# Routing half a chunk sooner, and the rows of the later dense groups mixed on other engines and turned in fp32r

## The chip, the cores and the metric

The kernel runs on one core of one Trainium2 chip. The metric is the device time of one execution in microseconds (us). Five engines run side by side, each with its own in-order queue: TensorE (PE, with its weight loads shown as PEld), VectorE (DVE), ScalarE (ACT), GpSimd (POOL) and SyncE (SP). Semaphores order them where one needs what another makes. DMAs are issued from the queues of SP, ACT and POOL.

## The reference

All in float32. Sliding-window attention of 4 batches, 8 heads, 576 positions and 64 values a head, so 2304 tokens of 512 values; then a layer of 8 experts, of which each token takes two; then a dense layer of two products with a gate between them.

```python
mask = (rel >= 0) & (rel < 64)                      # rel = query position - key position
x = softmax(where(mask, q @ k.T / 8, -1e9)) @ v     # -> x [2304, 512]
noisy = x @ w_gate + log1p(exp(x @ w_noise)) * noise
top2 = indices of the two largest of noisy; top2_w = their softmax
y[mask] += top2_w[mask, k] * (relu(x[mask] @ w1[e]) @ w2[e])     # for each expert e, k in (0, 1)
h = y @ w_in                                        # [2304, 2048]
g = where(h >= 1, h, where(h <= -1, 0, (h + 1) ** 2 / 4))
out = g @ w_out                                     # [2304, 512]
```

## The kernel before

Products are made in three fp32r matmuls: each operand is cut into a high half that fp32r holds and a low half with the rest, and high by high, low by high and high by low are summed in PSUM. A tile is typed fp32r or f32; PE transposes a tile in its own type. ACT copies the high half (`AF.Copy` into an fp32r tile) and DVE subtracts it for the low half: `split_w` and its second part `rest_w` for weights, `xpose` for rows of x.

The order of instructions is written out by hand; each engine's queue follows the order of the Python calls. There are three stages.

Attention and routing. `step(u)` runs for u = 0 to 36 (NU = 36), two steps for a tile of 128 tokens. It makes scores (`A`), a row maximum on DVE (`top`), exponentials on ACT (`soft`), transposes them (`C`), and every second step multiplies them with v (`Dm`), which ends with a normalization on DVE: `rl`, its reciprocal, and x = ov * rl (L406 to L409). Two steps later x is transposed (`Ex`) and the router's logits are made (`Gm`, in `logits`). Tiles are routed in groups of 8, 4 and 6. `route(g)` is a generator of many small DVE steps; `advance` lets each live one run to its next stop, and then makes up to 2 or 4 marks: for each choice a pair of one-hot tiles, `ohr` (L586) and `ohe` (L593 on DVE or L596 on ACT). `place` (L634) multiplies the pairs on PE into a PSUM bank that sums up each expert's list of tokens. As soon as the marks of the first two groups are placed, `early` reads that bank (L460 to L479), and POOL gathers the first three blocks of rows for expert 0 (`xg0a`, L732), so that expert 0 can start while the last six tiles are still being routed. `xpose` turns these rows (L759).

Experts. A unit is one expert, or for expert 0 two (`0a`, `0b`). Its eight chunks of 128 hidden values each have a first product (`do_mm1`, L891), a relu split into halves (ACT L899, DVE L902), and a second product (`do_mm2`, L964). The first product of the next chunk always stands ahead of the second product of this one. `rest = tail()` is the generator that finishes the routing of the last group beside expert 0: each call `more()` places what marks there are and advances `route(2)`; when all is placed it makes the lists, gathers the rows of `0b` and counts. The first four calls in the order before were: at the top of chunk 0, after the first product of chunk 1, after the second product of chunk 0, and at the top of chunk 1. The fifth, after the first product of chunk 2, issues the router's sums on PE (L558 to L562), which need `ohs` (L543).

Dense layer. Five groups of 2, 4, 4, 4 and 4 blocks of 128 tokens. `prep_gather` loads for each block the two rows that the experts made (y1, y2), the block is mixed as y1 * w0 + y2 * w1, turned by PE (`xturn`, L1236) and copied (`xcopy`, L1242). The first group uses plain products; the other four a Strassen scheme of seven products (`wino`, L1178), for which `xsums` makes four differences of quarters (L1255) and `xsplit` cuts seven operands into halves (L1265, L1267). The products go to two PSUM banks in turn; each is evicted by one or two DVE instructions, or one on ACT (L1159, L1163, L1168). `gate` follows (ACT L1196 and L1202, DVE L1197, L1200 and L1206). A group has eight items p, an item seven slots j; in slot (p, j) stand the j-th product of an item two ahead, a part of a gate and a seventh of the second products of this item. The preparation of the next group stands in slots named by hand. Groups 2, 3 and 4 are prepared under groups 1, 2 and 3, which are alike; group 1 is prepared under group 0, in another way that the diff leaves as it is.

Of the kernel before, what the change touches and what calls it, by code (L numbers as in the profile page):

```python
# [57 lines left out]
def fused_kernel(ctx, tc, qT, kT, v, wg, noise, wcat, out, wd=None):  # L58
# [617 lines left out]
    def step(u):  # L676
# [27 lines left out]
        if u % 2 == 1 and 0 <= m - 2 < NT:  # L704
            logits(m - 2, u)
        place()
        early()
        advance(MARKS[u > NU - 10])
        if 0 <= u - 1 < NU:
            Dm(u - 1)  # L710
# [40 lines left out]
    def xpose(key, b, m=P, TR=TR):  # L751
        if key not in xT:
            xT[key] = x_tiles(key, F32R)
        hi, lo = xT[key]
        t = gat.pop((key, b))

        o, i = (TR.bitcast(F32R), idr) if t.dtype == F32R else (TR, idn)
        for k in range(4):
            nc.tensor.transpose(o[:, k * P:k * P + m], t[0:m, k * P:k * P + P], i[0:m, 0:m])  # L759
        tv = TR.rearrange("p (k t) -> p k t", k=4)[:, :, 0:m]  # L760
        sl = slice(b * P, b * P + m)
        nc.scalar.activation(hi[:, :, sl], tv, AF.Copy)
        nc.vector.tensor_tensor(out=lo[:, :, sl], in0=tv, in1=hi[:, :, sl].bitcast(F32), op=ALU.subtract)
# [251 lines left out]
    def prep_gather(un, b):  # L1015
# [9 lines left out]
        else:  # L1025
            y = [pool["sc"].tile([P, DM], F32, tag="s", name=f"y{t}_{c}") for c in range(2)]
            eng = nc.gpsimd if un is units[FIRST2 + 1] else nc.sync
            for c in range(2):
                eng.dma_start(out=y[c], in_=yd[:, c, :])
        gat[un["key"], b] = (y, t)  # L1030

    def mix_two(un, b):
        (y1, y2), t = gat[un["key"], b]
        nc.scalar.activation(y1, y1, AF.Copy, scale=wts[:, t, 0:1])
        yield
        nc.vector.scalar_tensor_tensor(out=y2, in0=y2, scalar=wts[:, t, 1:2], in1=y1, op0=ALU.mult, op1=ALU.add)
        gat[un["key"], b] = y2

    def prep_mix(un, b):
# [190 lines left out]
    def xturn(ui, b):  # L1230
        un = units[ui]
        t = gat.pop((un["key"], b))
        free = [bank[7]] + [x for x in bank[2:7] if x not in units[ui - 1]["m2"]]
        held[ui, b] = to = free[b % len(free)]
        for k in range(4):
            nc.tensor.transpose(to[:, k * P:k * P + P], t[:, k * P:k * P + P], idn)  # L1236

# [7 lines left out]
    def xsums(ui, part=(0, 1, 2, 3)):  # L1245
# [7 lines left out]
        for i in part:  # L1253
            out, x, y = ((t1, b12, b11), (t2, b22, t1), (t3, b22, b12), (t4, b21, t2))[i]
            (nc.vector if d else nc.gpsimd).tensor_tensor(out=out, in0=x, in1=y, op=ALU.subtract)  # L1255
        if 3 in part:
# [27 lines left out]
    n64 = 2 * NF2  # L1284
    ndec = ndl = 0
    do_mm1(0)
    ndone = 1
    for s in range(len(seq)):
# [59 lines left out]
        if ui == 0:  # L1348
            more()
            if f == NF - 2:  # L1350
# [4 lines left out]
                rank(0)  # L1355
                prep_gather(units[2], 0)
                rank(1)
# [3 lines left out]
        do_mm2(s, ahead_xpose)  # L1361
        if s in (0, 2):
            rest_w(EW - 2 + s // 2, slice(0, 1024))
        if s == 0:
            more()
        for _ in range(SPLITS[ui][f] if ui in SPLITS else int(0 < ui < U7A)):
# [22 lines left out]
        if ui == U7B and f:  # L1389
# [4 lines left out]

    AT = ({(4, 0): (None,), (4, 4): (0,), (4, 5): (1,), (5, 0): (2,), (5, 1): (3,), (5, 3): (4,), (6, 2): (5,), (6, 3): (6,)},
          {})
# [13 lines left out]
    for q, (ui, p) in enumerate(items):  # L1410
# [22 lines left out]
        for j in range(7):  # L1433
            if nxt:
# [6 lines left out]
                if not late:  # L1441
                    if 1 <= p < 3 and j in (2, 4):
                        prep_mix(nxt, 2 * (p - 1) + j // 2 - 1)
                    if 2 <= p < 4 and j in (1, 3):
                        xturn(ui + 1, 2 * (p - 2) + j // 2)
                        xcopy(ui + 1, 2 * (p - 2) + j // 2)
                else:
# [6 lines left out]
                for x in AT[late].get((p, j), ()):  # L1454
                    xsums(ui + 1) if x is None else xsplit(ui + 1, x)
            if j < len(g):
# [40 lines left out]
```

## Time and profile before

| what | value |
|---|---|
| median of 3 runs | 954.07 us (952.11 to 954.48) |
| the profiled execution's own time | 953.95 us |
| its span, first to last instruction | 952.2 us |
| mean granted TensorE clock | 0.998 |
| PE busy | 938.4 us, 99% |
| DVE, ACT, POOL busy | 69%, 47%, 23% |

The span leaves out what lies before the first and behind the last instruction, 1.75 us here. Times in the rows count from the span's start. Busy time of PE is modelled at the ends of matmuls, so that a PE that is shown busy may still run below its rate; the distance from one start to the next tells more. In brackets stands how long the engine had been idle and what ended it.

### The profile page before, as it was taken

The numbers are of one execution on the slowest core, as the hardware profiler recorded it, in microseconds if no ns is written. First come the engines' busy times: TensorE is split into PE (matmuls) and PEld (weight loads), VectorE is DVE, ScalarE is ACT, GpSimd is POOL, SyncE is SP. The second block draws the span as 40 slices with busy tenths as digits, with TensorE's granted clock in tenths as the row PEclk, the third lists the DMA queues.
The fourth block names the chain that finished last, engine by engine and source line by source line (L and its number), as shares of the span: only waits on it lengthen the run. The fifth ranks groups of instructions, "written<-read, shape, count | busy, mean of one in ns | idle before, by whom it ended". The sixth has DMA issues, their size and how long they took to land. (4 is left out here: it accounts for less than half of the span.)

```text
span 952.2 us, 18037 instructions
## 1 busy us (share of the span) xinstructions
PE 938.4 (99%) x6779; PEld 832.8 (87%) x6781; DVE 659.5 (69%) x1386; ACT 444.3 (47%) x920; POOL 222.1 (23%) x273
## 2 busy tenths in 40 slices
PE   9999899999999999999999999999999999999998
PEld 6887788988889889889888889988998899899997
DVE  5688665477997968889543377766766777677664
ACT  7897325345565555555432366343334334442221
POOL 4222013133544353354402030013002201300000
PEclk9999999999999999999999999999999999999999
DMA  8884126555888777767626567775586458556521
GB/s 269 289 271 150 50 89 195 187 194 198 285 287 285 256 233 278 258 211 250 244 89 202 201 212 254 256 235 175 177 273 208 149 173 306 174 176 207 188 94 44
DMA packets 91274, 196.95 MB, mean 207 GB/s; under 512 B 7320, under 2 KB 18072, under 8 KB 91184
## 3 DMA queue, kind: packets, MB, share of 16 engines
q1 hardware_dynamic: 83152, 171.68, 54.4%
q0 software_dynamic: 6736, 21.86, 6.4%
q10 hardware_dynamic: 1296, 2.23, 0.6%
q8 instruction: 54, 0.88, 0.4%
q14 instruction: 36, 0.29, 0.1%
HBM read 155.45 MB, written 40.29 MB: 206 GB/s over the span
## 5 line engine op out<-in xcount | busy, mean ns | idle before, releaser
L964 PE MATMUL bank<-wo,hall 128*128 128x512 f32 x864 | 237.6, 394 | 0.0
L964 PE MATMUL bank<-w,hall 128*128 128x512 f32 (+3 forms) x944 | 236.2, 398 | 0.1
L964 PEld LDWEIGHTS bank<-w,hall 128*128 128x128 f32 (+3 forms) x944 | 168.8, 185 | 35.5 <-issue 0.3
L964 PEld LDWEIGHTS bank<-wo,hall 128*128 128x128 f32 x864 | 146.7, 188 | 17.4 <-DVE hall L910 0.2
L899 ACT ACTIVATE hall<-bank 128x288 fp32r<-128x288 f32 (+6 forms) x128 | 54.0, 422 | 219.7 <-PE bank L891 197.3
L891 PE MATMUL bank<-xhie,w 128*128 128x288 f32 (+4 forms) x768 | 122.6, 302 | 0.5 <-DVE hall L902 0.4
L891 PEld LDWEIGHTS bank<-xhie,w 128*128 128x128 f32 x768 | 113.5, 188 | 7.5 <-DVE hall L902 1.3
L902 DVE SCALAR_TENSOR_TENSOR hall<-bank,hall 128x288 fp32r<-128x288 f32 (+7 forms) x168 | 59.9, 390 | 84.3 <-ACT hall L899 76.2
L149 DVE TENSOR_TENSOR w<-raw,w 128x1024 fp32r<-128x1024 f32 (+1 forms) x69 | 82.0, 1188 | 23.7 <-ACT w L158 19.4
L1178 PEld LDWEIGHTS bank<-xb,wi 128*128 128x128 f32 x576 | 80.5, 188 | 10.1 <-DVE cg L1168 1.2
L1202 ACT ACTIVATE hall<-cg 128x512 fp32r<-128x512 f32 x64 | 40.3, 629 | 100.5 <-DVE cg L1200 100.5
L1178 PE MATMUL bank<-xb,wi 128*128 128x256 f32 x576 | 84.7, 282 | 0.6 <-DVE cg L1168 0.3
L1178 PEld LDWEIGHTS bank<-xc,wi 128*128 128x128 f32 x480 | 67.2, 188 | 7.6 <-DVE wg L1163 0.6
L1178 PE MATMUL bank<-xc,wi 128*128 128x256 f32 x480 | 70.2, 281 | 0.2 <-DVE wg L1163 0.2
L1045 POOL TENSOR_TENSOR y<-y,y 128x512 f32<-128x512 f32 x14 | 19.1, 1365 | 217.1 <-ACT y L1044 217.1
L158 ACT ACTIVATE w<-raw 128x1024 fp32r<-128x1024 f32 (+1 forms) x71 | 69.4, 977 | 0.0
L891 PE MATMUL bank<-xloe,w 128*128 128x288 f32 (+4 forms) x384 | 69.1, 302 | 0.0
L204 POOL TENSOR_TENSOR td<-rawd 128x512 f32<-128x512 f32 x32 | 33.3, 1040 | 139.7 <-DVE rawd L202 111.8
L1196 ACT ACTIVATE mg<-cg 128x512 f32<-128x512 f32 x64 | 40.1, 626 | 46.8 <-DVE cg L1168 45.1
L1197 DVE SCALAR_TENSOR_TENSOR cg<-mg,cg 128x512 f32<-128x512 f32 x64 | 46.9, 733 | 18.8 <-ACT mg L1196 18.8
L891 PEld LDWEIGHTS bank<-xloe,w 128*128 128x128 f32 x384 | 58.0, 188 | 0.0
L1206 DVE SCALAR_TENSOR_TENSOR hall<-cg,hall 128x512 fp32r<-128x512 f32 x64 | 45.9, 717 | 9.1 <-ACT hall L1202 8.7
(284 smaller groups left out, 1442.8 us busy)
## 6 DMA issues: line engine op xcount, KB each, us to landing
wi<-w1o SPq DMA_DIRECT2D x56, 1024.0 KB
raw<-wcat SPq DMA_DIRECT2D x64, 512.0 KB
rawd<-wd SPq DMA_DIRECT2D x32, 512.0 KB
w1o<-so SPq DMA_DIRECT2D x64, 256.0 KB
y<-y_dram SPq DMA_DIRECT2D x28, 256.0 KB
vE<-v SPq DMA_DIRECT2D x18, 260.0 KB
x_dram<-x SPq DMA_DIRECT2D x18, 256.0 KB
k<-kT SPq DMA_DIRECT2D x8, 512.0 KB
```

Source lines behind the costliest of these rows:

```text
L149: nc.vector.tensor_tensor(out=w[:, 1, c], in0=t[:, c], in1=w[:, 0, c].bitcast(F32), op=ALU.subtract)
L158: nc.scalar.activation(w[:, 0, c], t[:, c], AF.Copy)
L204: nc.gpsimd.tensor_tensor(out=t, in0=hf, in1=lf, op=ALU.add)
L891: nc.tensor.matmul(ps, lhsT=l[k], rhs=r[:, k, s:s + w], start=(c == 0), stop=(c == len(prods) - 1))
L899: nc.scalar.activation(hh, ps, AF.Relu)
L902: nc.vector.scalar_tensor_tensor(out=t, in0=ps[:, c], scalar=0.0, in1=hh[:, c].bitcast(F32), op0=ALU.max, op1=ALU.subtract)
L964: nc.tensor.matmul(M2[b][0:w], lhsT=h2[:, o:o + w], rhs=r[n], start=(first and a == 0), stop=(last and a == end))
L1178: nc.tensor.matmul(ps, lhsT=w[:, l, k * P:k * P + P], rhs=r[:, m, k, :], start=(c == 0), stop=(c == len(prods) - 1))
L1196: nc.scalar.activation(st["m"], c, AF.Relu, scale=0.5)
L1197: nc.vector.scalar_tensor_tensor(out=c, in0=st["m"], scalar=1.0, in1=c, op0=ALU.min, op1=ALU.subtract)
L1202: nc.scalar.activation(h2[:, 0:T], c, AF.Copy, scale=-1.0)
L1206: nc.vector.scalar_tensor_tensor(out=h2[:, T:2 * T], in0=c, scalar=-1.0, in1=h2[:, 0:T].bitcast(F32), op0=ALU.mult, op1=ALU.subtract)
```

## The change

Five edits. (1) In the last steps of the attention, `place` is left out of step 33, so that its marks are placed in step 34, and in step 32 `Dm` stands ahead of `advance` and its marks. (2) The high half of the first gathered block is copied on DVE instead of ACT. (3) `more()` is called once ahead of the first product of chunk 0 instead of behind its second product, and the two `rest_w` of chunks 5 and 6 follow it there, instead of standing behind the second products of chunks 0 and 2. (4) The second block of expert 1's rows is gathered together with the first, between the two calls of `rank`. (5) For groups 2 to 4, y1 lies in a tile typed fp32r. `mix_copy` takes the place of `prep_mix`: one scaling on ACT, a multiply-add on DVE into y2 (three or four slots later), and a DMA from POOL's queue that copies y2 over y1; PE then turns y1 in fp32r. `xsums` is always made on DVE, one difference in each of four slots, where POOL made all four at (4, 0). The turns move from slots (2,1), (2,3), (3,1), (3,3) to (2,3), (2,5), (3,3), (3,4).

```diff
@@ -703,10 +703,13 @@
 
         if u % 2 == 1 and 0 <= m - 2 < NT:
             logits(m - 2, u)
-        place()
+        if u != NU - 3:
+            place()
         early()
+        if u == NU - 4:
+            Dm(u - 1)
         advance(MARKS[u > NU - 10])
-        if 0 <= u - 1 < NU:
+        if 0 <= u - 1 < NU and u != NU - 4:
             Dm(u - 1)
 
         for c in range(EW):
@@ -759,7 +762,10 @@
             nc.tensor.transpose(o[:, k * P:k * P + m], t[0:m, k * P:k * P + P], i[0:m, 0:m])
         tv = TR.rearrange("p (k t) -> p k t", k=4)[:, :, 0:m]
         sl = slice(b * P, b * P + m)
-        nc.scalar.activation(hi[:, :, sl], tv, AF.Copy)
+        if (key, b) == ("0a", 0):
+            nc.vector.tensor_copy(hi[:, :, sl], tv)
+        else:
+            nc.scalar.activation(hi[:, :, sl], tv, AF.Copy)
         nc.vector.tensor_tensor(out=lo[:, :, sl], in0=tv, in1=hi[:, :, sl].bitcast(F32), op=ALU.subtract)
 
     for u in range(NU + 1):
@@ -1023,10 +1029,11 @@
             nc.gpsimd.dma_start(out=y, in_=yd)
             y = [y[:, c] for c in range(2)]
         else:
-            y = [pool["sc"].tile([P, DM], F32, tag="s", name=f"y{t}_{c}") for c in range(2)]
+            wide = un is not units[FIRST2] and un is not units[FIRST2 + 1]
+            y = [pool["sc"].tile([P, DM], F32R if wide and c == 0 else F32, tag="s", name=f"y{t}_{c}") for c in range(2)]
             eng = nc.gpsimd if un is units[FIRST2 + 1] else nc.sync
             for c in range(2):
-                eng.dma_start(out=y[c], in_=yd[:, c, :])
+                eng.dma_start(out=y[c].bitcast(F32) if y[c].dtype == F32R else y[c], in_=yd[:, c, :])
         gat[un["key"], b] = (y, t)
 
     def mix_two(un, b):
@@ -1035,6 +1042,15 @@
         yield
         nc.vector.scalar_tensor_tensor(out=y2, in0=y2, scalar=wts[:, t, 1:2], in1=y1, op0=ALU.mult, op1=ALU.add)
         gat[un["key"], b] = y2
+
+    def mix_copy(un, b):
+        (y1, y2), t = gat[un["key"], b]
+        nc.scalar.activation(y2, y2, AF.Copy, scale=wts[:, t, 1:2])
+        yield
+        nc.vector.scalar_tensor_tensor(out=y2, in0=y1.bitcast(F32), scalar=wts[:, t, 0:1], in1=y2, op0=ALU.mult, op1=ALU.add)
+        nc.gpsimd.dma_start(out=y1.bitcast(F32), in_=y2)
+        gat[un["key"], b] = y1
+        yield
 
     def prep_mix(un, b):
         if un["e"] is None:
@@ -1232,8 +1248,9 @@
         t = gat.pop((un["key"], b))
         free = [bank[7]] + [x for x in bank[2:7] if x not in units[ui - 1]["m2"]]
         held[ui, b] = to = free[b % len(free)]
+        o, i = (to.bitcast(F32R), idr) if t.dtype == F32R else (to, idn)
         for k in range(4):
-            nc.tensor.transpose(to[:, k * P:k * P + P], t[:, k * P:k * P + P], idn)
+            nc.tensor.transpose(o[:, k * P:k * P + P], t[:, k * P:k * P + P], i)
 
     def xcopy(ui, b):
         if b == 0:
@@ -1252,7 +1269,7 @@
         b11, b21, b12, b22 = (f[:, i] for i in range(4))
         for i in part:
             out, x, y = ((t1, b12, b11), (t2, b22, t1), (t3, b22, b12), (t4, b21, t2))[i]
-            (nc.vector if d else nc.gpsimd).tensor_tensor(out=out, in0=x, in1=y, op=ALU.subtract)
+            nc.vector.tensor_tensor(out=out, in0=x, in1=y, op=ALU.subtract)
         if 3 in part:
             staged[ui] = (b11, b21, t2, t3, t4, t1, b22)
 
@@ -1283,6 +1300,9 @@
     nload = NF + 2
     n64 = 2 * NF2
     ndec = ndl = 0
+    more()
+    for c in (EW - 2, EW - 1):
+        rest_w(c, slice(0, 1024))
     do_mm1(0)
     ndone = 1
     for s in range(len(seq)):
@@ -1353,16 +1373,13 @@
                 for b in range(nxt["nb"]):
                     prep_xpose(nxt, b, (TR, bank[6])[b])
                 rank(0)
-                prep_gather(units[2], 0)
+                for b in range(2):
+                    prep_gather(units[2], b)
                 rank(1)
         if ui == U7A and f == 2:
             overflow(nc.values_load(cnt_i[0:1, 0:1], min_val=0, max_val=16 * N))
             pool["x4"] = ffn.enter_context(tc.tile_pool(name="x4", bufs=1, reuse_waits="tile"))
         do_mm2(s, ahead_xpose)
-        if s in (0, 2):
-            rest_w(EW - 2 + s // 2, slice(0, 1024))
-        if s == 0:
-            more()
         for _ in range(SPLITS[ui][f] if ui in SPLITS else int(0 < ui < U7A)):
 
             if nsplit == SP:
@@ -1392,7 +1409,9 @@
                 load_out(f + 2)
     assert ndec == n64 and nsplit == nload == N2
 
-    AT = ({(4, 0): (None,), (4, 4): (0,), (4, 5): (1,), (5, 0): (2,), (5, 1): (3,), (5, 3): (4,), (6, 2): (5,), (6, 3): (6,)},
+    mixes = deque()
+    TURN2, SUM2 = [(2, 3), (2, 5), (3, 3), (3, 4)], [(3, 6), (4, 0), (4, 6), (5, 0)]
+    AT = ({(4, 4): (0,), (4, 5): (1,), (5, 0): (2,), (5, 1): (3,), (5, 3): (4,), (6, 2): (5,), (6, 3): (6,)},
           {})
     TURN, COPY = {(3, 0): (0,), (3, 1): (1,), (3, 6): (2,), (4, 0): (3,)}, {(3, 3): (0, 1), (4, 2): (2, 3)}
     g1 = FIRST2 + 1
@@ -1440,10 +1459,15 @@
                     prep_gather(nxt, 2 * p + j)
                 if not late:
                     if 1 <= p < 3 and j in (2, 4):
-                        prep_mix(nxt, 2 * (p - 1) + j // 2 - 1)
-                    if 2 <= p < 4 and j in (1, 3):
-                        xturn(ui + 1, 2 * (p - 2) + j // 2)
-                        xcopy(ui + 1, 2 * (p - 2) + j // 2)
+                        mixes.append(mix_copy(nxt, 2 * (p - 1) + j // 2 - 1))
+                        next(mixes[-1])
+                    if (p, j) in ((1, 6), (2, 0), (2, 6), (3, 0)):
+                        next(mixes.popleft())
+                    if (p, j) in TURN2:
+                        xturn(ui + 1, TURN2.index((p, j)))
+                        xcopy(ui + 1, TURN2.index((p, j)))
+                    if (p, j) in SUM2:
+                        xsums(ui + 1, (SUM2.index((p, j)),))
                 else:
                     for b in TURN.get((p, j), ()):
                         xturn(ui + 1, b)
@@ -1452,7 +1476,7 @@
                     if p == 4 and j > 4:
                         xsums(ui + 1, (0, 1) if j == 5 else (2, 3))
                 for x in AT[late].get((p, j), ()):
-                    xsums(ui + 1) if x is None else xsplit(ui + 1, x)
+                    xsplit(ui + 1, x)
             if j < len(g):
                 g[j]()
             if gen:
```

## Rows read from the trace of the kernel before

**Rows 1.** Page: busy us, share of the span and instructions, by engine.
```profile
PE 938.4 (99%) x6779; PEld 832.8 (87%) x6781; DVE 659.5 (69%) x1386; ACT 444.3 (47%) x920; POOL 222.1 (23%) x273
```
**Rows 2.** Timeline of PE, 107 to 125: start, us, instructions [idle before, releaser].
```profile
107.29 2.24 PE L964 MATMUL bank<-w,hall 128*128 128x512 f32 x9
...
113.53 0.18 PE L558 MATMUL bank<-ohs,tri 128*128 128x48 bf16 x1 [1.89 <-DVE ohs L543]
...
113.70 3.89 PE L964 MATMUL bank<-w,hall 128*128 128x512 f32 x9
```
**Rows 3.** Timeline of DVE, 102 to 118.
```profile
102.98 0.69 DVE L763 TENSOR_TENSOR xlo0a<-bank,xhi0a 128x512 fp32r<-128x512 f32 x1 [0.97 <-ACT xhi0a L762]
...
108.01 0.56 DVE L902 SCALAR_TENSOR_TENSOR hall<-bank,hall 128x384 fp32r<-128x384 f32 x1 [1.19 <-ACT hall L899]
...
110.28 1.22 DVE L149 TENSOR_TENSOR w<-raw,w 128x1024 fp32r<-128x1024 f32 x1
...
113.27 0.21 DVE L543 TENSOR_TENSOR ohs<-o 128x48 bf16<-128x48 f32 x1
...
117.73 0.26 DVE L593 TENSOR_SCALAR ohe<-io,rf 128x145 f16<-128x145 f16 x1
```
**Rows 4.** Windows: length, busy of PE, PEld, DVE, ACT, POOL; clock; DMA share; GB/s.
```profile
106.40:113.48 7.08, 5.24 (x28) 4.62 (x27) 5.58 (x34) 2.41 (x5) 0.00 (x0) 1.00 0.00 0
115.00:120.00 5.00, 5.00 (x25) 4.30 (x24) 2.88 (x14) 1.01 (x3) 0.00 (x0) 0.77 0.01 3
```
**Rows 5.** Timeline of all engines, 86 to 104.
```profile
89.91 0.25 DVE L593 TENSOR_SCALAR ohe<-io,rf 128x145 f16<-128x145 f16 x1
...
90.50 0.69 DVE L409 TENSOR_TENSOR x<-ob,rl 128x512 f32<-128x512 f32 x1
...
91.34 0.63 PE L422 MATMUL bank<-idn,x 128*128 128x128 f32 x4 [0.76 <-DVE first L460]
...
95.27 0.95 POOL L732 DMA_INDIRECT xg0a<-x_dram,src_i  x1 [0.30 <-issue]
...
101.67 0.64 PE L759 MATMUL bank<-idr,xg0a 128*128 128x128 f32 x4
```
**Rows 6.** Timeline of PE, 624 to 659: the first products of items.
```profile
624.32 0.87 PE L1178 MATMUL bank<-xb,wi 128*128 128x256 f32 x6
...
634.87 0.87 PE L1178 MATMUL bank<-xb,wi 128*128 128x256 f32 x6
...
646.30 0.87 PE L1178 MATMUL bank<-xb,wi 128*128 128x256 f32 x6
...
658.52 0.74 PE L1178 MATMUL bank<-xb,wi 128*128 128x256 f32 x4 [0.16 <-DVE wg L1163]
```
**Rows 7.** Timeline of DVE and POOL, 652 to 659; and line L1255 on DVE (ns, min/median/max).
```profile
654.28 0.41 DVE L1163 TENSOR_TENSOR tg<-bank,ug 128x256 f32<-128x256 f32 x1
654.62 1.46 DVE L1200 SCALAR_TENSOR_TENSOR cg<-mg,cg 128x512 f32<-128x512 f32 x1
...
655.49 1.75 POOL L1255 TENSOR_TENSOR xd<-xf 128x512 f32<-128x512 f32 x1
...
L1255 DVE TENSOR_TENSOR xlos<-xhis x2: 683/683/683, 589.0 to 590.3; 128x512 f32<-128x512 f32 x2
```
**Rows 8.** DMA queues in the window 97.3 to 99.4: packets, MB, share of 16 engines.
```profile
q0 software_dynamic: 79, 0.26, 43.9%
```
**Rows 9.** Timeline of POOL, 562 to 569: loads behind the last expert's scatters.
```profile
568.02 1.53 POOL L1023 DMA_DIRECT2D y<-y_dram  x2 [4.74 <-DMA y_dram<-y7b,rank_i]
```
**Rows 10.** Timeline of PE around two turns, fp32r and f32.
```profile
192.35 0.46 PE L759 MATMUL bank<-idr,xge 128*128 128x128 f32 x4
192.64 0.47 PE L964 MATMUL bank<-w,hall 128*128 128x512 f32 x1
...
723.07 0.60 PE L1236 MATMUL bank<-idn,y 128*128 128x128 f32 x4
723.42 0.93 PE L1178 MATMUL bank<-xc,wi 128*128 128x256 f32 x6
```

## Prediction

> **What bounds the kernel now.** I read the page first, then the timeline of each engine around the edits, in order of time. The page shows PE busy for 99% of the span [rows 1], so an edit gains only what it takes out of PE's own stream, and the question is where that stream stands still or runs slowly beside an edit. There are three such places.
>
> First, the end of the routing. PE waits 1.89 us for `ohs`, the expert choices of the last six tiles, which DVE makes [rows 2, 3]. What follows runs slowly: nine matmuls that took 2.24 us one chunk earlier take 3.89 us, and the granted clock over 115 to 120 us is 0.77, between the levels of 2.4 and 1.2 GHz; PE had stood idle just before [rows 2, 4].
>
> Second, the end of the attention. A transposition waits 0.76 us: its input x is normalised only after DVE has made the marks of that step (the last ends at 90.16, x at 91.19) [rows 5].
>
> Third, the dense groups. An item of seven products with POOL sums in it takes 658.52 - 646.30 = 12.22 us, one without them 634.87 - 624.32 = 10.55 us [rows 6]. Two turns of 0.44 us (worked out in term 3) stand in the longer one; 0.79 us is left over. DVE shows why: while a POOL sum runs, a gate instruction with both inputs in SBUF takes 1.46 us, where a DVE instruction of that size takes 0.68 us without POOL; one with an input in PSUM keeps its 0.41 us [rows 7]. The evictions of PE's two banks queue behind the slow ones.
>
> **Term 1, routing sooner.** `more()` is now called once ahead of the first hidden product, and the two `rest_w`, 1.22 us each [rows 3], follow it there. From the fourth call on nothing moves, so the work that makes `ohs` stands at the same place of PE's stream; what goes is DVE's delay. In the 7.08 us up to 113.48, when `ohs` ends, DVE waited 1.19 us for a relu [rows 3, 4]; the other 5.89 us are work, with one `rest_w` in it. The new order adds the other `rest_w` and the first eviction of hidden rows, 0.56 us: 7.67 us. It starts when the last half-split ends, 102.98 + 0.69 = 103.67 [rows 3], where DVE sat idle for the first relu. So `ohs` is ready at 111.3 us, and PE asks for it at 113.53 - 1.89 = 111.64 [rows 2]. The wait goes: 1.9 us. With it goes the slow stretch, if PE's idling brought it: 3.89 - 2.24 = 1.6 us.
>
> The stall does not vanish whole: the marks are late next. From `ohs` to the end of the first four marks DVE took 117.99 - 113.48 = 4.51 us [rows 3]; from 111.3 this ends at 115.8, and up to 1 us later, since on the way it must wait for the third chunk's relu and for a copy on ACT, neither of which comes sooner. PE asks for these marks one chunk after 111.64, a chunk being 111.64 - 107.29 = 4.35 us [rows 2], at 116.0. So a wait between 0 and 0.9; I take 0.7, since both waits on ACT are certain. Term 1 is 1.9 + 1.6 - 0.7 = 2.8 us, with bounds of 1.2 (the clock stays low) and 3.5. The first eviction comes about 1 us later, near 107.0; its reader is the third matmul after 107.29 [rows 2], so this costs nothing as it stands, and what DVE is late beyond 0.7 us otherwise.
>
> **Term 2, end of the attention.** With `Dm` ahead of the marks x is ready some 1.2 us sooner, and at most the 0.76 us of idle time goes, with a little at the next one. But the marks end 1.2 us later, and with them the small copy behind them that frees a PSUM bank for PE; and the skipped `place()` lets a step's transpositions go first, so that the gathers of the first experts' rows start some 1.3 us later. POOL began the last one at 95.27; its queue still moves packets in 97.3 to 99.4 us; PE reads the rows at 101.67 [rows 5, 8]. 1.3 us later they are there at 100.7, still ahead, but this caps the gain at about 1 us. Of the half-copy that goes from ACT to an idle DVE under 0.1 us reaches the path. I take 0.5 us, halfway. The bounds are 0.9 and -0.6, the latter if the last gather takes as long as the last scatter of rows 9: 4.74 us after an issue of 0.95 us [rows 5], so that 96.6 + 5.7 = 102.3 passes 101.67.
>
> **Term 3, turns in one pass.** Four f32 transpositions hold PE from 723.07 to 723.42, 0.35 us, and stretch the six matmuls behind them from 0.87 to 0.93 us and their successors a little: 0.44 in all. Four fp32r ones hold it 192.64 - 192.35 = 0.29 us [rows 6, 10]. That is 0.06 us or a little more for each of twelve turns: 0.8 us, bounds 0.7 and 0.9.
>
> **Term 4, sums on DVE.** Three groups lose 0.79 us each in that item and a little in the one beside it, 2.4 to 2.7 us; I take 2.5. Against it DVE gets four sums of 0.68 us [rows 7] and four mixes of that kind per group, 5.5 us in 86 us. They stand in eight slots of some 1.5 us (a seventh of an item), not four in a row, and each slot's eviction may be late by about a slot before PE asks for its bank. That covers one instruction of 0.68 us, not two. Bounds: 0, when DVE is as late as with POOL, and 2.7. ACT loses twelve scalings. The gather for the next expert's second block goes ahead of three scatters on POOL's queue and delays each by one issue, 0.95 us [rows 5]; nobody reads them before the mixes, hundreds of us later: nothing.
>
> The Trainium skill, page SBUF — State Buffer, section Who interferes with whom, says that a DVE instruction with two SBUF inputs contends with a GpSimd one that reads SBUF, and one with a single SBUF input does not. The trace agrees: 1.46 against 0.68 us, and 0.41 us unchanged [rows 7]. By that rule the whole loss goes with the POOL sums, and the term would be 2.7 us.
>
> **Sum.** 2.8 + 0.5 + 0.8 + 2.5 = 6.6 us off the profiled execution's 953.95 us: 947.3 us. The median of the runs is 954.07, 0.12 us away; nothing is corrected for it.
>
> **Rivals.**
> *The clock still falls.* PE now waits near 116 us for the marks, in several short pieces. If that brings the slow stretch, 1.6 us stays: 948.9 us. For it: there the clock fell behind an idle PE. Against it: the wait of 0.76 us at 91 us was followed by no slow stretch. 0.13.
> *DVE becomes the limit in the dense groups.* Where a sum, a split and a gate meet in one slot, evictions are late again; term 4 falls to nothing: 949.8 us. Against it stands the spacing. 0.09.
> *The attention's end loses,* since the gathers come later: -0.6 instead of 0.5, 948.4 us. 0.05.
> *The copies on POOL's queue are late (the side of slower).* Each mixed block is copied within SBUF by a POOL DMA, and its turn comes four slots later, some 6.5 us (in one of four, five slots). The mix takes 0.7 us and starts about when its slot does, so 5 to 5.8 us are left for issue and copy. The last gather needed at most 99.4 - 95.27 = 4.1 us beside other traffic [rows 5, 8], so no turn waits. At the scatter's 5.7 us [rows 5, 9] the tightest turn waits 0.7 us in each group: 949.4 us. A later turn's lateness is partly taken up by an earlier one's wait, so about two of four count in full. From 6.4 us on they wait 2.2 us a group, which eats the whole gain; at 7.3 us, 4 us a group, 959.3 us. What could bring it there is the weight loads, which use the same DMA engines. 0.13, of which 0.07 is slower, 0.04 no change and 0.02 faster.
> The skill's same page, section SBUF: two separate sides, says that descriptors of a POOL DMA wait while DVE holds the shared port pair. No row here shows it for a plain copy; by it each copy would start one DVE instruction later.
> *Two of these together,* with no change to measure: 0.03.
>
> **How the numbers follow.** The forecast has the remaining 0.57. A measurement of this kernel can tell about 0.3% (2.9 us) from no change, so faster means below 951.2 us: 0.57 + 0.13 + 0.09 + 0.05 + 0.02 = 0.86. No change is 0.04 + 0.03 = 0.07, slower 0.07. The range: all terms at their upper bounds (3.5 + 0.9 + 0.9 + 2.7 = 8.0) give 945.9, and small waits that vanish beside them bring 945.5. At the other end it takes in each single miss up to the lost sums at 949.8, and 0.6 us more, 950.4. Outside are the late copies, the double miss and a few hundredths below.
>
> **What would show it.** Right: no PE wait on L558, a clock of 1.0 over 105 to 125 us, short waits for marks instead; no POOL sum after 600 us, gates at 0.68 us throughout, items of 10.6 us plus turns; 0.29 us from a turn to the next matmul. Wrong: PE idle ahead of a turn with the copy as its releaser; a slow stretch of the clock behind the marks; PE waiting for evictions in the slots of the sums; a first expert matmul later than 103.0 us.

## The result and the profile after

The changed kernel took 957.71 us, the median of 6 runs (956.33 to 960.6), beside 952.23 us for the kernel before, the median of 6: a ratio of 1.0054, 95% interval 1.0035 to 1.0073. It is slower by 0.5%. The forecast was 947.3 us, faster. Run once more without an edit (f1), it came out at 1.0066 (1.0044 to 1.0088).

The profiled execution took 960.6 us, with a span of 958.9 us. First the waits of PE: line, what it waited for, us in total, times, the longest.

```profile
PE bank L1253 <- DMA y<-y: 5.2, 4, 1.7
PE bank L762 <- DMA xg0a<-x_dram,src_i: 4.7, 1, 4.7
...
PE bank L634 <- DVE ohe L593: 0.9, 5, 0.3
...
PE bank L422 <- ACT pt L389: 0.5, 1, 0.5
PE bank L558 <- ACT pt L389: 0.3, 1, 0.3
```

The old first entry, 1.9 us on `ohs`, is gone. The 0.76 us behind the marks at 91 us [rows 5] have become 0.55 us at the same transposition (L422), which now waits for `pt` from ACT; a wait of 0.86 us for x one step later, at 96.06 us before, is gone. Two new ones of 9.9 us in all stand ahead of everything else. L1253 is the transposition in `xturn`: it waits for the copies. L762 is the one in `xpose`: it waits for the gathered rows of expert 0.

**The end of the attention.** The timeline of PE, then that of POOL:

```profile
98.15 0.53 PE L762 MATMUL bank<-idr,xg0a 128*128 128x128 f32 x4
98.52 0.63 PE L422 MATMUL bank<-idn,x 128*128 128x128 f32 x4
103.83 0.75 PE L762 MATMUL bank<-idr,xg0a 128*128 128x128 f32 x4 [4.69 <-DMA xg0a<-x_dram,src_i]
...
108.29 3.04 PE L897 MATMUL bank<-xhi0a,w 128*128 128x384 f32 x8
...
111.88 1.56 PE L897 MATMUL bank<-xhi0a,w 128*128 128x384 f32 x8
...
113.97 2.24 PE L970 MATMUL bank<-w,hall 128*128 128x512 f32 x9
...
118.17 0.20 PE L558 MATMUL bank<-ohs,tri 128*128 128x48 bf16 x1
...
118.36 2.29 PE L970 MATMUL bank<-w,hall 128*128 128x512 f32 x9
```

```profile
94.00 1.24 POOL L735 DMA_INDIRECT xg0a<-x_dram,src_i  x1 [4.00 <-DVE src_i L476]
...
96.82 0.95 POOL L735 DMA_INDIRECT xg0a<-x_dram,src_i  x1 [0.30 <-issue]
```

The last gather begins at 96.82 us, 95.27 before [rows 5]. PE turns the first block and then stands still for 4.69 us for the second. Eight products take 3.04 us behind that, and 1.56 us two lines on: half the clock. The windows show it (us, five engines' busy time, granted clock, DMA share, GB/s):

```profile
100.00:105.00 5.00, 1.17 (x8) 1.17 (x8) 0.14 (x1) 0.38 (x1) 0.00 (x0) 0.59 0.29 106
105.00:110.00 5.00, 5.00 (x20) 3.89 (x21) 3.05 (x7) 1.30 (x4) 0.00 (x0) 0.50 0.00 0
110.00:115.00 5.00, 5.00 (x26) 4.83 (x25) 3.31 (x11) 0.98 (x2) 0.00 (x0) 0.89 0.00 0
115.00:120.00 5.00, 5.00 (x32) 4.38 (x31) 3.43 (x26) 1.44 (x2) 0.00 (x0) 1.00 0.00 0
```

At the next stage all is as forecast: L558 starts without a wait for `ohs`, and the nine products behind it take 2.29 us where they took 3.89 [rows 2].

**The dense groups.** The timeline of PE around the first two turns of a group; the tile `y` on DVE and POOL (ns, min/median/max, first and last start) with the time from a copy's issue to its landing; SP's queue; and two windows.

```profile
640.77 1.09 PE L970 MATMUL bank<-wo,hall 128*128 128x512 f32 x4
643.49 0.54 PE L1253 MATMUL bank<-idr,y 128*128 128x128 f32 x4 [1.62 <-DMA y<-y]
...
646.98 0.46 PE L1253 MATMUL bank<-idr,y 128*128 128x128 f32 x4
647.27 0.95 PE L1194 MATMUL bank<-xa,wi 128*128 128x256 f32 x6
```

```profile
L1050 DVE SCALAR_TENSOR_TENSOR y<-y,wts,y x2: 743/744/744, 635.8 to 636.9; 128x512 f32<-128x512 f32 x2
L1051 POOL DMA_DIRECT2D y<-y x2: 539/540/542, 637.2 to 638.2; - x2
...
DMA to landing us min/median/max: 5.9/6.1/6.3
```

```profile
636.51 0.37 SPq L1129 DMA_DIRECT2D wi<-w1o  x1
```

```profile
638.00:640.00 2.00, 2.00 (x14) 1.78 (x13) 1.26 (x4) 1.42 (x3) 0.54 (x1) 1.00 0.83 222
640.00:642.00 2.00, 1.87 (x11) 1.30 (x10) 1.08 (x3) 0.21 (x1) 0.00 (x0) 1.00 1.01 308
```

The sum of a block runs at 635.8, its copy is issued at 637.2, and it lands 6.3 us later; its turn, due at 641.9, waits. SP has issued a weight load of 1 MB 0.7 us ahead of the copy, and over 638 to 642 us the DMA engines are busy for a share of 0.83 and then 1.01. The second turn, at 646.98, waits for nothing, and its next matmul comes 0.29 us on, as forecast. In the second of the three groups the wait costs more than its length:

```profile
731.03 0.54 PE L1253 MATMUL bank<-idr,y 128*128 128x128 f32 x4 [1.69 <-DMA y<-y]
...
734.61 1.62 PE L970 MATMUL bank<-wo,hall 128*128 128x512 f32 x4
736.07 0.46 PE L1253 MATMUL bank<-idr,y 128*128 128x128 f32 x4
```

From this turn to the next PE takes 5.04 us, where it took 3.49 us in the group above; four matmuls take 1.62 us instead of 1.09. The granted clock is 0.58 over 732 to 734 us and 0.56 over 734 to 736 us. Behind the waits of the other two groups, 1.62 and 1.61 us long, it stays at 1.00.

The sums on DVE do what was forecast. One line of the gates on DVE from 600 us on, L1200 of before (ns, min/median/max, first and last start):

```profile
L1216 DVE SCALAR_TENSOR_TENSOR cg<-mg,cg x60: 678/686/694, 609.2 to 928.5; 128x512 f32<-128x512 f32 x60
```

None of the sixty takes more than 0.69 us, where one beside a POOL sum took 1.46 [rows 7].

### The profile page after: what moved, and what is told of

It is laid out like the page before. It is cut to its first block, busy times and chain, and to the rows that moved or that the text cites. A ratio compares the mean times of both kernels' runs of the same rounds, so it can differ in the third digit from the quotient of the medians.

```text
span 958.9 us, 18048 instructions
## 1 busy us (share of the span) xinstructions
PE 940.0 (98%) x6781; PEld 835.3 (87%) x6781; DVE 666.0 (69%) x1411; ACT 437.0 (46%) x907; POOL 191.7 (20%) x261
## 5 line engine op out<-in xcount | busy, mean ns | idle before, releaser
L1218 ACT ACTIVATE hall<-cg 128x512 fp32r<-128x512 f32 x64 | 40.3, 630 | 99.4 <-DVE cg L1216 99.4
L1213 DVE SCALAR_TENSOR_TENSOR cg<-mg,cg 128x512 f32<-128x512 f32 x64 | 43.8, 685 | 23.6 <-ACT mg L1212 23.6
L1051 POOL DMA_DIRECT2D y<-y x12 | 6.5, 538 | 248.9 <-DVE cg L1184 170.7
L1222 DVE SCALAR_TENSOR_TENSOR hall<-cg,hall 128x512 fp32r<-128x512 f32 x64 | 43.9, 686 | 7.4 <-ACT hall L1218 7.0
```

Of the source, the lines that this page charges most:

```text
L1213: nc.vector.scalar_tensor_tensor(out=c, in0=st["m"], scalar=1.0, in1=c, op0=ALU.min, op1=ALU.subtract)
L1218: nc.scalar.activation(h2[:, 0:T], c, AF.Copy, scale=-1.0)
L1222: nc.vector.scalar_tensor_tensor(out=h2[:, T:2 * T], in0=c, scalar=-1.0, in1=h2[:, 0:T].bitcast(F32), op0=ALU.mult, op1=ALU.subtract)
```

## The experiments

All times below are medians; a ratio stands against the kernel before on the same chip, with its 95% interval. "Step order" is the edit at the end of the attention, "sooner copies" an edit of mine.

| kernel | us | ratio |
|---|---|---|
| changed | 957.71 | 1.0054 (1.0035 to 1.0073) |
| f1, changed, once more | 961.18 | 1.0066 (1.0044 to 1.0088) |
| e1, old step order | 958.21 | 1.0052 (1.0034 to 1.0070) |
| i3, the same once more | 955.02 | 1.0025 (1.0011 to 1.0039) |
| e2, sooner copies | 952.49 | 0.9988 (0.9974 to 1.0001) |
| e3, old step order, sooner copies | 949.54 | 0.9955 (0.9939 to 0.9972) |
| i2, the same once more | 946.65 | 0.9941 (0.9927 to 0.9955) |
| e4, no copies, turns in f32 | 953.47 | 1.0001 (0.9991 to 1.0010) |
| f2, before with the routing part alone | 952.51 | 0.9973 (0.9959 to 0.9986) |
| f3, sooner copies, normalization ahead only | 951.60 | 0.9962 (0.9950 to 0.9975) |
| f4, sooner copies, placing skipped only | 953.34 | 0.9984 (0.9970 to 0.9999) |
| h1, e3 with the second gather in its old place | 945.79 | 0.9927 (0.9913 to 0.9940) |
| i1, the same once more | 946.81 | 0.9946 (0.9931 to 0.9961) |
| h2, before with the pair of gathers alone | 953.15 | 1.0004 (0.9994 to 1.0013) |
| h3, old step order, copies on ACT's queue | 951.50 | 0.9991 (0.9982 to 1.0000) |
| i4, h1 with the old routing | 948.81 | 0.9966 (0.9953 to 0.9979) |

**The changed kernel once more (f1).** No edit.

> The changed kernel once more, unedited, on the same chip as the next three and with a profile of its own. Theory: its loss has two parts, rows late at the end of the attention (some 3 us or more, wait and half clock) and copies late at the first turn of each dense group (over 5 us); the ratio to before is 1.005 again and both waits are in the profile, the first of them of another length. Rival: the long wait for gathered rows was an accident of one execution; then it is absent and only the copies remain.

```profile
PE bank L1253 <- DMA y<-y: 5.3, 4, 1.7
PE bank L762 <- DVE xloe L769: 2.2, 1, 2.2
...
PE bank L762 <- DMA xg0a<-x_dram,src_i: 1.1, 1, 1.1
```

Both waits are there again. The copies' is the same to 0.1 us; the one for rows is 1.1 us and not 4.7, so its length belongs to the execution, not its being there. The second line is a wait that the first profile did not have; it comes up again below.

**The step order taken back (e1).**

```diff
-        if u != NU - 3:
-            place()
+        place()
         early()
-        if u == NU - 4:
-            Dm(u - 1)
...
-        if 0 <= u - 1 < NU and u != NU - 4:
+        if 0 <= u - 1 < NU:
```

> The changed kernel with the last attention steps in the old order (placing not skipped, normalization behind the marks); all else as changed. Theory: the later gathers are the whole loss at the end of the attention. Then the PE wait of 4.7 us for gathered rows goes, the 10.2 us at half clock behind it (5 us lost) go too, and the 1.3 us that the new order had gained are given back: about 6 to 8 us off, near 951 us. Rival: the rows come late because instruction packets and stores of x cross them wherever they stand; then the wait stays and the time is 958 to 959 us.

The wait for gathered rows is gone from the profile. The median did not follow: 958.21 us, 1.0052, the rival's time without its cause. What is left, in the profile, are 5.5 us of waits at the turns and the 2.1 us at expert 1's rows; that waits can cost more than they are long is seen above and in i3, below.

**The copies sooner (e2).** Each sum and copy runs two slots sooner, some 3 us.

```diff
-                    if (p, j) in ((1, 6), (2, 0), (2, 6), (3, 0)):
+                    if (p, j) in ((1, 4), (1, 5), (2, 4), (2, 5)):
                         next(mixes.popleft())
```

> The changed kernel with the second half of every dense mix (sum and copy) two slots sooner, some 3 us, the turns where they are. Theory: the copies need 6.3 us from issue to landing, so 3 us more cover them: the four PE waits (5.2 us) and the half clock at 732 us (1.6 us) go, about 6.8 us off, near 951 us. Rival: the copies' packets wait for the weight loads, whose time is set by the items and not by the copy's issue; then they land no sooner, and the time stays near 957 us.

952.49 us, and no PE wait for a copy in the profile: the theory's mechanism. Of the 6.8 us expected, 5.2 are off by the medians and 6.3 by the ratios (1.0054 and 0.9988). Left at the end of the attention is a wait for rows of 0.5 us and a granted clock of 0.66 in both 100 to 105 and 105 to 110 us.

**Both (e3).**

> The changed kernel with both edits: old order of the last attention steps, and the dense sums and copies two slots sooner. Theory: the two losses are apart in time and add up, so some 13 us come off and the kernel runs at 945 to 946 us, faster than before by 0.7%. Rival: one of the two losses stays, 951 us; or the sooner copies delay the weight loads, 948 to 950 us.

949.54 us: faster than before, but 4 us short. The profile has neither wait, and a PE wait of 2.1 us at the second turn of expert 1's rows (L759, put down to `xloe` on DVE) that the kernel before had as 0.5 us.

**No copies (e4).** Rows are turned in f32 again. The mixes are made by `mix_two`, as for group 1 in the kernel before: a scaling on ACT and a multiply-add on DVE, in the slots of the change and without a copy. The sums stay on DVE.

```diff
-            wide = un is not units[FIRST2] and un is not units[FIRST2 + 1]
+            wide = False
...
-                        mixes.append(mix_copy(nxt, 2 * (p - 1) + j // 2 - 1))
+                        mixes.append(mix_two(nxt, 2 * (p - 1) + j // 2 - 1))
                         next(mixes[-1])
...
-                        next(mixes.popleft())
+                        next(mixes.popleft(), None)
```

> The changed kernel without the copies: the dense mixes in the same slots, sums of differences on VectorE as changed, rows turned in f32 as before. Theory: the waits at the turns belong to the copies alone, and a turn in f32 costs 0.07 us more: 957.7 - 6.8 + 0.8 = 951.7 us, and no PE wait at a turn or for an eviction. Rival: VectorE's sums make the turns and evictions late; then waits of some us stay in the dense groups and the time is over 954 us.

953.47 us, between the theory's 951.7 and the rival's 954, with no PE wait at a turn or for an eviction in the slots of the sums: the waits belong to the copies. It sizes two terms. The item that held POOL's sums takes 658.21 - 646.80 = 11.41 us here, 12.22 before [rows 6]; with fp32r turns it takes 11.29 us (in i2, below).

**The step order, one half at a time (f3, f4).** Both have the sooner copies. f3 keeps the normalization ahead of the marks and places in every step; f4 skips the placing and normalizes behind the marks.

> The changed kernel with the sooner copies, and of the step order only the normalization ahead of the marks; placing is not skipped. Theory: the marks, 1.2 us later on VectorE, make the gathers late; then PE waits for gathered rows as with both, and the time is that of the sooner copies with the new order, a ratio of 0.999. Rival: the skipped placing makes them late; then no wait, some of the 0.8 us wait at 91 us gone, and 0.995 or a little less.

> The changed kernel with the sooner copies, and of the step order only the skipped placing; the normalization stays behind the marks. Theory: the marks' delay makes the gathers late and not the placing; then no wait for rows and a ratio of 0.995. Rival: the skipped placing puts the gathers a part of a step later; then PE waits for rows, the clock falls, and the ratio is 0.999.

Both rivals came true, though f3, at 0.9962, gains a little less than its rival said. The turns of expert 0's rows on PE, in f3 and then in f4:

```profile
100.69 0.64 PE L761 MATMUL bank<-idr,xg0a 128*128 128x128 f32 x4
101.55 0.53 PE L761 MATMUL bank<-idr,xg0a 128*128 128x128 f32 x4
```

```profile
98.76 0.54 PE L760 MATMUL bank<-idr,xg0a 128*128 128x128 f32 x4
101.69 0.75 PE L760 MATMUL bank<-idr,xg0a 128*128 128x128 f32 x4 [0.88 <-DMA xg0a<-x_dram,src_i]
```

Executions lead or lag by up to 1.6 us before the first edit, so I shift each timeline until one product of the attention (81.53 us in the kernel before) coincides:

| kernel | shift | last gather begins | first turn | second turn | first product of expert 0 |
|---|---|---|---|---|---|
| before | 0 | 95.27 | 98.88 | 99.74 | 103.00 |
| changed | 0.45 | 96.37 | 97.70 | 103.38 | 107.84 |
| f1, changed | 0.39 | 96.37 | 97.65 | 100.92 | 105.39 |
| e3, old order | 1.37 | 95.26 | 98.62 | 99.48 | 102.74 |
| f3, normalization ahead | 1.63 | 95.61 | 99.05 | 99.91 | 103.17 |
| f4, placing skipped | 0.43 | 96.89 | 98.33 | 101.26 | 105.72 |

Skipping a `place()` makes the last gather 1.6 us later (f4 against e3), since the step whose marks complete the list is placed one step later, and brings PE to its first turn sooner. Normalizing ahead alone costs 0.4 us, at the first product of expert 0.

**The routing part alone (f2).** To the kernel before:

```diff
     ndec = ndl = 0
+    more()
+    for c in (EW - 2, EW - 1):
+        rest_w(c, slice(0, 1024))
     do_mm1(0)
...
         do_mm2(s, ahead_xpose)
-        if s in (0, 2):
-            rest_w(EW - 2 + s // 2, slice(0, 1024))
-        if s == 0:
-            more()
```

> The kernel before with one part of the change alone: the router's steps and the last two weight halves ahead of the first hidden product. Theory: the stall of 1.9 us and the slow stretch of 1.6 us go, as predicted, but some 1.6 us are given back where the next expert's first rows are turned, since a wait stands there that grew from 0.5 to 2.1 us in the last four runs: 1.5 to 2 us off in the end, a ratio of 0.998. Rival: nothing is given back, 3 us off, 0.997; or everything, 1.000.

0.9973, 2.6 us off by the ratio: nearly the rival's 3 us. Expert 1's rows wait 0.5 us, as before.

**The pair of gathers (h1, h2).** h1 is e3 with the line `for b in range(2)` ahead of `prep_gather(units[2], b)` taken back; h2 is the kernel before with that line.

> The changed kernel with three of its edits taken back or mended: old order of the last attention steps, dense sums and copies two slots sooner, and the gather of the next expert's second block back in its old place, behind the scatters. Theory: the pair of gathers brought the PE wait of 2.1 us at the second turn of expert 1's rows, since the kernel with the routing part alone keeps a wait of 0.5 us there; then 1.6 us come off the 0.9955 of the kernel with both mended, 0.9940. Rival: the wait comes with PE's being sooner, whatever the gathers do; then it stays at 2.1 us and 0.9955.

> The kernel before with the pair of gathers alone. Theory: the wait at the second turn of expert 1's rows grows from 0.5 to 2.1 us and the kernel is 1.6 us slower, 1.0017. Rival: no change, 1.000, and a wait of 0.5 us.

h1 is at 0.9927 without the wait of 2.1 us; but h2, with the pair, has not even the 0.5 us, and 1.0004. So the pair alone does not bring the wait. Whether it has a part in it, these two do not tell: h3, on the same chip, has the pair and the sooner routing together, as e3 has, and no such wait either.

**The copies on ACT's queue (h3).** To e1:

```diff
-        nc.gpsimd.dma_start(out=y1.bitcast(F32), in_=y2)
+        nc.scalar.dma_start(out=y1.bitcast(F32), in_=y2)
```

> The changed kernel with the old step order, and the copies issued from ScalarE's queue in place of GpSimd's, in the slots of the change. Theory: what makes a copy late is the traffic of the weight loads on the same DMA engines, so it lands some 6 us after its sum again and PE waits over 5 us at the turns, 1.005 as before this edit. Rival: GpSimd's issue and its queue make it late (0.65 us from the sum to the issue, 0.54 us for the issue itself, packets that come late); then the copies land over 1.5 us sooner, the waits shrink below 2 us in all, and the ratio is 0.998 or less.

Waits of PE, then the tile `y` in 622 to 642 us:

```profile
PE bank L1250 <- DMA y<-y: 4.4, 3, 1.6
```

```profile
L1048 ACTq DMA_DIRECT2D y<-y x2: 472/496/520, 630.2 to 631.3; - x2
...
DMA to landing us min/median/max: 6.4/6.6/6.8
```

The issue follows the sum by 0.1 us, and the copy lands as late as from POOL's queue: 6.4 to 6.8 against 5.9 to 6.3 us. The first turn of each group still waits. The profile speaks for the theory: the traffic, not POOL, makes the copies late. The ratio does not: 0.9991 is nearer to the rival's 0.998 than to the theory's 1.005. Against e1 (1.0052) and i3 (1.0025) the kernel gains more than the 0.8 to 1.1 us by which its waits are shorter, and what else the other queue saves is not shown. The Trainium skill, page DMA: Bandwidth & Descriptors, section Issuing engines are not separate DMA queues, says that transfers issued by any engine run on the same 16 DMA engines and interleave; the landing times from the two queues agree with that.

**Four together on one chip (i1 to i4).** i1 is h1, i2 is e3, i3 is e1, each unedited. i4 is h1 with the routing where it stood before (the diff of f2 backwards).

> The version that ran at a ratio of 0.9927 (old step order, sooner copies, second gather of the next expert in its old place), once more, beside the next three on one chip. Theory: 0.993 again and no PE wait over 0.3 us between the first expert and the end. Rival: its 0.9927 owed some 2 us to the chip that it ran on; then 0.995 and a wait of some 2 us at expert 1's rows.

> The same with the pair of gathers kept, as changed (old step order, sooner copies). Theory: the wait of 2.1 us at expert 1's rows is the pair's where it follows the sooner routing; then it is here and not in the kernel beside it, and the ratio is 0.002 higher. Rival: it goes by the chip and not by the pair, since two kernels with the pair had no such wait in the last call; then both have it or neither, and the ratios agree within 0.001.

i1 and i2 agree, 946.81 and 946.65 us, and neither has the wait at expert 1's rows: the rival of i2. i1's ratio, 0.9946, is nearer to its rival's 0.995, but without the wait. The wait came up in all seven profiles with the pair on two of the chips (those of the e and f runs), and in none of the other five with the pair. f2, the one profile without the pair on those two chips, has 0.5 us there.

> The changed kernel with the old step order and the copies late as changed, once more. Theory: the two losses add up, and by the first runs the late copies alone cost 8.7 us (958.2 against 949.5 with sooner copies), so a ratio near 1.003 where the best version has 0.993. Rival: the first run stood high by its chip; the waits at the turns are 5.5 us, and with some of the slow clock 6 to 7 us stand between the two: 0.9995 to 1.001.

```profile
PE bank L1250 <- DMA y<-y: 5.2, 4, 1.7
```

955.02 us, 1.0025, near the theory, and 8.4 us above i2, of which 5.2 are these waits. Most of the rest is the clock: the three executions with a mean granted clock of 1.000 took 952.3 to 952.7 us, some 6 us above i2, and those with 0.994 and 0.995 took 956.5 and 958.1 us.

> The best version with the routing part taken back (the router's steps and the last weight halves where they stood before). Theory: the routing part is worth its 2.6 to 3.3 us, so 0.9957 to 0.9962 here beside 0.993, and the stall of 1.9 us with its slow stretch is back. Rival: the gain is given back later; then 0.993 to 0.994.

```profile
113.54 0.18 PE L558 MATMUL bank<-ohs,tri 128*128 128x48 bf16 x1 [1.89 <-DVE ohs L543]
113.71 2.29 PE L967 MATMUL bank<-w,hall 128*128 128x512 f32 x9
...
118.31 2.33 PE L967 MATMUL bank<-w,hall 128*128 128x512 f32 x9
```

948.81 us, 2.0 us above i1, where the theory had 2.6 to 3.3. The stall of 1.89 us is back, but in this execution the nine products behind it take 2.29 us, not 3.89.

## Why the prediction was wrong

**Term 1, routing: right in its mechanism.** The stall goes, and the marks are late instead. In i1 the nine products behind the router's sums and the next nine begin at

```profile
111.78 2.29 PE L967 MATMUL bank<-w,hall 128*128 128x512 f32 x9
...
117.00 2.35 PE L967 MATMUL bank<-w,hall 128*128 128x512 f32 x9
```

so 5.22 us apart, and 118.31 - 113.71 = 4.60 us apart in i4: the marks cost 0.6 us, in pieces of at most 0.3 us, where 0.7 was taken. From the first product of expert 0 to the second products three chunks on it is 121.84 - 103.12 = 18.72 us in i1 and 123.14 - 103.03 = 20.11 us in i4: 1.4 us with the clock at full speed in both. The part is worth 2.0 us by the medians of i4 and i1, and 2.6 us by f2's ratio, where 2.8 was said. The term counted the slow stretch of 1.6 us in full. In i4 the same stall came without it, and in h2 with it (3.87 us for the nine products, a clock of 0.76 over 115 to 120 us): it follows some of these stalls and not others, and what decides is open.

**Term 2, end of the attention: this step failed.** It forecast gathers 1.3 us later (1.1 measured) with the rows there "at 100.7, still ahead". Three things were wrong in that. The check was made for the last block and its turn at 101.67 alone; the second block is turned at 99.74 and had less to spare. These are the first two turns and the first product of expert 0 in the kernel before:

```profile
98.88 0.65 PE L759 MATMUL bank<-idr,xg0a 128*128 128x128 f32 x4
...
99.74 0.53 PE L759 MATMUL bank<-idr,xg0a 128*128 128x128 f32 x4
...
103.00 1.68 PE L891 MATMUL bank<-xhi0a,w 128*128 128x384 f32 x8
```

The consumer was left where it was, though the same edit lets PE come 1.2 us sooner (98.88 to 97.70): the margin shrank by both shifts, 2.3 us. And the lower bound of -0.6 us priced a late row as a wait only, while PE's idling was followed by half the clock: the first product of expert 0 came 4.8 us late in the first profile and 2.4 us late in f1, and in the first profile its first eight products took 1.4 us more, at half clock (3.04 against 1.68). Between e2 and e3, on one chip, the step order cost 2.95 us. Even the old order has little to spare: in i1 the third turn waits 0.66 us.

The wait was 4.7 us once and 1.1 us another time largely because the gather itself was slow once: in the first profile the second block landed 8.3 us after its issue, while in f1 its turn began 5.8 us after the issue, and the gathers of expert 0's rows in h1 to h3 and i1 to i4 took 3.5 to 6.4 us. Why it was slow is not settled. The DMA view of 101.6 to 104 us of that profile is nearly empty:

```profile
DMA packets 15, 0.04 MB, mean 16 GB/s; under 512 B 7, under 2 KB 7, under 8 KB 14
...
q0 software_dynamic: 6, 0.02, 3.0%
q8 instruction: 1, 0.02, 2.6%
```

PE waited over 2 us for the last six packets of gathers, in a stretch with one packet of instructions. That the six stood behind that one on their DMA engine would explain it, but no row names the engine of a packet.

**Term 3, turns: right.** 0.29 us from a turn to the next matmul. The item with two turns takes 11.41 us in f32 (e4) and 11.29 in fp32r (i2), 0.06 us a turn, some 0.75 us for twelve.

**Term 4, sums on DVE: right.** No item waits for an eviction in the slots of the sums, and the item takes 12.22 - 11.41 = 0.81 us less, 2.4 us for three groups where 2.5 was taken. In i2, items of two turns follow each other at

```profile
631.23 0.87 PE L1191 MATMUL bank<-xb,wi 128*128 128x256 f32 x6
...
642.51 0.87 PE L1191 MATMUL bank<-xb,wi 128*128 128x256 f32 x6
...
653.80 0.87 PE L1191 MATMUL bank<-xb,wi 128*128 128x256 f32 x6
```

11.28 and 11.29 us: plain items of 10.55 us [rows 6] with two turns.

**The rival of the late copies: it happened, and its chance of 0.13 was the second failure.** It had the place, the cause (weight loads on the same DMA engines) and nearly the price of the waits right: 0.7 us a group at a landing of 5.7 us and 2.2 us at 6.4. Measured were 5.9 to 6.3 us at the first pair of a group, 1.6 to 1.7 us of waits in each of three groups, and another in one of them, 5.2 us in all. The clock that falls behind a wait was not in its price; with it the copies cost 8.4 us (i3 - i2). What failed is the step that held the gather's 4.1 us against it, so "no turn waits". That gather ran at 95 us in another stage; a copy of the same stage has to be held against what SP issues there, 1 MB of weights an item. With the sum and copy two slots sooner no turn waits. The rival of two misses together, at 0.03, is what happened, late copies and a late end of the attention; it was priced at no change, since the slow clock was in neither part.

**Both together.** 2.95 us for the order and 8.4 us for the copies are 11.4 us; 957.7 less that is 946.3 us, and the version without both losses runs at 945.8 to 946.8 us, 0.5 to 0.7% faster than before. This adds differences from different chips, and one pair does not fit: e1 and the changed kernel, which differ by the order alone, stand at 1.0052 and 1.0054, where i3, the same kernel as e1, is at 1.0025. Against the kernel before on the same chip, h1, i1 and i2 are 6.9, 5.3 and 5.4 us faster; the forecast's terms 1, 3 and 4, which they keep, make 6.1 us. So these gains were there, and two tardy transfers ate them. The part of the step order that normalizes ahead did not help either (f3 against e3: first product 0.4 us later), so the best version leaves the attention's end as it was.

**Not settled:** the wait of 2.1 us at expert 1's rows. The pair of gathers alone does not make it, since five profiles with the pair are without it. But on the two chips that show it all seven profiles with the pair have it, and f2, without the pair, has 0.5 us, so the pair may have a part in it. The traces of these two chips also hold fewer landings of DMAs, 6509 to 6763 against 7312 to 7504 in the h and i runs; whether that has to do with it is not known. The rows of the wait put it down to an operand that DVE made late, behind a relu that ACT began at 152.68 us in e3, 3.9 us after the start of the last product that it reads; nothing in the trace says what ACT waited for.

## What to carry to other kernels

When an edit moves a producer later, check every consumer, the second as well as the last, at the time at which it would run if nothing held it; an edit that frees the consumer spends the margin from the other side. Take the time of a transfer from one in the same stage, beside the loads that are issued there; a copy that nobody measured deserves a slot or two of slack, beside which no new wait showed here. A wait of PE can cost more than itself, since the clock may fall behind it.

## What the runs showed of the hardware

In the changed kernel a copy of 256 KB within SBUF took 6.3 us from issue to landing when a 1 MB load had been issued 0.7 us ahead of it, and 5.9 to 6.0 us when it followed the load by 1.6 to 1.7 us; one issued 1.1 us ahead of such a load landed in 2.3 us:

```profile
L1051 POOL DMA_DIRECT2D y<-y x1: 539/539/539, 650.2 to 650.2; - x1
...
DMA to landing us min/median/max: 2.3/2.3/2.3
```

The same stall of PE, 1.89 us at the same instruction, was followed by a granted clock of 0.77 over 115 to 120 us in the kernel before [rows 4], by 0.76 in h2, and by 1.00 in i4. Of three waits of 1.6 to 1.7 us at the turns of the changed kernel, one was followed by a clock of 0.58 and 0.56 over the next 4 us and two by 1.00.
